# New table of priorities for one large fused kernel (attention, gated feed-forward, routed experts)

## The chip, the cores and the metric

The kernel runs on one core of one Trainium2 chip. The metric is the device time of one execution in microseconds (us). The engines are TensorE (PE, with its weight loads as PEld), VectorE (DVE), ScalarE (ACT), GpSimd (POOL) and SyncE (SP, which issues most transfers).

## What the kernel computes

Three layers in a row, on 2304 tokens. The first is attention by random features, for 4 batches of 8 heads:

```python
q_p, k_p = phi(q * scale), phi(k * scale)   # exp(x @ omega.T - |x|^2/2 - max), 128 features
num = einsum('bhsm,bhmd->bhsd', q_p, einsum('bhsm,bhsd->bhmd', k_p, v))
x = num / (einsum('bhsm,bhm->bhs', q_p, sum_s(k_p)) + 1e-6)      # 2304 x 512
```

The second is a gated feed-forward with 1536 hidden units, and the third sends each token to one of eight experts:

```python
xn = x / rms(x) * rms_g
x = (silu(xn @ w_gate) * (xn @ w_val)) @ w_out                    # 512 -> 1536 -> 512
e = argmax(x @ w_gate2 + bias[modality])                          # and its softmax weight
out = gate_w * (relu(x @ w1[e]) @ w2[e])                          # 512 -> 1024 -> 512
```

## The kernel before

The tokens are worked through in **chunks**. For each chunk PE makes the features (L675), the sums of keys times values (L765) and the numerators with their denominators (L943). DVE divides (L961 to L970). The root of the mean square follows: squares on ACT (L990), the power on POOL (L995, L996), and the scaling of the row either on DVE (L1002, one instruction) or on POOL (L1006 and L1007). The scaled x is then split into a coarse and a fine half-precision part and turned, so that the model dimension lies on the partitions: early chunks by PE (L1320), chunks 4 and later by two transposing transfers that SP issues (L1350). The queries of the later chunks are turned by transfer as well (L624).

**Feed-forward.** The hidden gemm (L1364) fills one half of a PSUM bank of gate and value with twelve matmuls, a *dozen*; two dozens make a unit. Its epilogue is ACT's tanh (L1383), DVE's (tanh+1)*g (L1388) and the product that empties the bank (L1410 on DVE; in early chunks, while the weights come, L1397 on ACT and L1402 on POOL or DVE). The product is split again into a coarse cast (L326 on ACT, L332 on DVE) and a rest (L336), and the output projection (L1434, three matmuls to a triple) reads both. A bank can be filled again only when its L1410 has read it.

**Weights.** In the first 190 us the weights are brought from 64-bit numbers to 32-bit ones and split in two. DVE does the step on the bits in three instructions per tile (L1049, L1056, L1064), and the halves are made by L1028 and L1034 on DVE or ACT. From then on L1028 and L1034 split the weights of the experts, which go out to memory and come back.

**Routing.** Each chunk's logits (L1500, then L1520 to L1542 on DVE) end in its largest expert. Partway through the last chunks the kernel already picks the experts (L1735 to L1762 on DVE, L1771 on PE, L1776 to L1793 on DVE), and after the last it counts ranks and writes a table (L2076, L2089). The experts run with L2312 and L2341 from about 580 us on.

**Spares.** 140 small matmuls on constants (L520), whose results nobody reads, are taken by PE whenever nothing else is ready by the plan.

**What sets the order.** All of this is entered step by step into a `Plan`: each step has an engine (or several to choose from), a planned cost and a wish time `want`. Then `schedule` replays the planned costs and hands every idle engine the ready step of least `want`; that order is what the engines are given, and the chip waits where a step isn't ready in fact. PSUM banks and buffers are given out in the same replay. Before it begins, the rows of `NUDGES` (L55 to L71) shift the wishes:

```python
for first, last, shift, *kind in NUDGES if self.nudged else ():
    for o in self.ops[first : last + 1]:
        if not kind or o.kind in kind:
            o.want += shift
```

A row thus names a range of steps, in the order in which they were entered, a shift, and perhaps one kind of step.

Of the kernel before, what the change touches and what calls it, by code (L numbers as in the profile page):

```python
# [52 lines left out]


NUDGES = (  # L55
    (933, 2761, 6.75, 63), (247, 724, 6.5, 39), (250, 359, -10.75), (0, 1732, 5.5, 7),
    (583, 596, 7.5), (105, 1477, -1.25, 63), (1339, 1364, 3.5), (1353, 1418, 1),
    (1155, 2378, 0.75, 63), (1484, 1548, 1.75), (365, 1101, 17, 32), (2622, 2634, 19.5),
    (713, 744, 14), (1455, 1458, -11.5), (547, 1849, 1.5, 41), (2080, 2406, 17, 40),
    (2046, 2134, 4.5, 41), (1730, 1875, 12.5, 86), (208, 215, -16.75), (1318, 1327, 10),  # L60
    (180, 1260, -1, 9), (123, 857, -9.75, 35), (125, 198, -6.25, 6), (2069, 2083, 1.75),
    (1753, 1763, -7.25), (698, 1599, -8.5, 8), (1925, 3163, 3, 73), (1354, 1356, 20),
    (1397, 1405, 0.25), (2260, 2303, 8.5), (631, 834, 5.25, 21), (145, 174, -3.75, 7),
    (1139, 1184, -5), (489, 494, 8), (2544, 2572, 5), (384, 811, -18.5, 51), (1948, 1977, 5.25, 88),
    (164, 660, -4.25, 29), (1979, 2623, 7, 81), (774, 1927, 3.5, 9), (2252, 2277, -2.75, 80),
    (517, 1281, -2.25, 29), (391, 446, 0.5), (314, 410, -7, 32), (621, 621, -3.5),
    (486, 505, -0.75), (1112, 1113, 8.75), (568, 1395, 0.25, 63), (748, 1137, 3, 9),
    (1402, 1723, -0.5, 87), (183, 1838, -2.5, 28), (1887, 3256, -8, 122), (2241, 2350, -9.5, 41),
    (1442, 1449, -2.5), (1734, 2390, -1.5, 9), (1122, 1126, 7.25), (252, 275, 8.75),
    (2065, 2080, -0.25), (1804, 1873, -1.5, 45), (2515, 2954, 0.75, 63), (2586, 2633, -8),  # L70
)  # L71


# [2388 lines left out]
```

## Time and profile before

| | us |
|---|---|
| median of 3 runs (807.05 to 809.35) | 807.44 |
| time of the profiled execution | 809.51 |
| its span | 807.8 |
| PE busy in the span | 785.0 |
| DVE busy | 564.6 |
| ACT busy | 476.3 |
| POOL busy | 337.5 |

The profiled execution took 1.71 us more than its span, which lies around it, and 2.07 us more than the median. A row that gives a group of instructions has their busy time, the mean of one in ns, and the idle time of the engine just before them with what ended it. In rows in order of time the first number is the start from the beginning of the span, the second how long the stretch of equal instructions took, and a bracket at the end says how long the engine had been idle and which step of which engine ended that.

### The profile page before, as it was taken

The page shows a single profiled execution, that of the slowest core. Times are in us where ns is not written, and L with a number is a line of the kernel's source. Part 1 is how long each engine was busy: PE and PEld are TensorE (multiplying, and loading weights), DVE is VectorE, ACT ScalarE, POOL GpSimd, SP SyncE. Part 2 cuts the span into 40 slices and gives each one's busy share as a digit, 9 for nine tenths or more (in the row PEclk, how much of TensorE's full clock was granted, in tenths as well). Part 3 has the DMA queues.
Part 4 walks back from the last instruction along what each step waited for, and adds up shares of the span by engine and source line. Part 5 has one row for each costly group of instructions (what it writes and reads, how often), then busy time and mean ns, then how long its engine had stood idle before and what let it go on. Part 6 is the DMA issues. An engine that isn't in the chain of part 4 may idle for free.

```text
span 807.8 us, 20366 instructions
## 1 busy us (share of the span) xinstructions
PE 785.0 (97%) x8042; PEld 613.5 (76%) x8042; DVE 564.6 (70%) x1295; ACT 476.3 (59%) x1138; POOL 337.5 (42%) x475
## 2 busy tenths in 40 slices
PE   9999999899999999999999999998999999999995
PEld 8998888788665776877768787777686777777772
DVE  5889899898455889999998999879667222222220
ACT  5767577686635787897877976676242332323231
POOL 0367898664222466545543755322222212222100
PEclk9999999999989999999999999999999999999998
DMA  8436340448213699977789999873826989999960
GB/s 289 166 99 229 112 151 28 131 148 293 82 42 79 184 274 253 277 256 229 248 260 282 265 265 298 269 235 131 320 88 268 405 306 399 415 405 417 418 274 30
DMA packets 69830, 188.25 MB, mean 233 GB/s; under 512 B 36927, under 2 KB 37055, under 8 KB 53856
## 3 DMA queue, kind: packets, MB, share of 16 engines
q1 hardware_dynamic: 66720, 177.27, 65.5%
q0 software_dynamic: 3008, 9.61, 3.1%
q8 instruction: 65, 1.06, 0.5%
q14 instruction: 37, 0.30, 0.1%
HBM read 135.96 MB, written 43.16 MB: 222 GB/s over the span
## 4 chain that ended last, share of the span: by engine, by line
PE 71%; DVE 12%; issue 6%; DMA 4%; POOL 4%; ACT 1%; SPq 0%; POOLq 0%; DVEq 0%; ACTq 0%
PE bank L1364 25%; PE bank L1434 16%; PE bank L2312 8%; PE bank L2341 7%; PE bank L675 4%; PE bank L765 4%; DMA out_dram<-plain,x 2%; DVE big L1028 2%; PE bank L943 2%; PE bank L520 1%; POOL plain L1402 1%; POOL big L336 1%; PE bank L1473 1%; DMA big<-in_w_moe_dram 1%; DVE plain L1388 1%
## 5 line engine op out<-in xcount | busy, mean ns | idle before, releaser
L1364 PE MATMUL bank<-x,big 128*128 128x256 f16 x2592 | 305.9, 273 | 4.7 <-DVE plain L1410 4.4
L1364 PEld LDWEIGHTS <-big 128*128 128x128 f16 x2592 | 251.4, 98 | 49.5 <-issue 7.5
L1434 PE MATMUL bank<-big 128*128 128x512 f16 x648 | 158.0, 382 | 0.0
L336 POOL TENSOR_TENSOR big<-plain,big 128x256 f16<-128x256 f32 (+1 forms) x118 | 107.7, 915 | 110.3 <-ACT big L326 82.6
L1028 DVE SCALAR_TENSOR_TENSOR big<-big,e_fac 128x512 f16<-128x512 f32 x128 | 107.2, 848 | 2.3 <-ACT big L1034 1.5
L1434 PEld LDWEIGHTS <-big 128*128 128x128 f16 x648 | 62.2, 100 | 56.1 <-issue 2.4
L2312 PEld LDWEIGHTS <-big 128*128 128x128 f16 x1632 | 96.0, 98 | 10.6
L2312 PE MATMUL bank<-plain,big 128*128 128x128 f16 x1632 | 101.6, 219 | 0.0
L2341 PE MATMUL bank<-big,plain 128*128 128x512 f16 x408 | 98.5, 379 | 0.0
L1249 ACT ACTIVATE plain<-big,plain 128x1024 bf16<-128x1024 f32 x64 | 73.1, 1142 | 7.0 <-DMA big<-in_w_exp_dram 6.8
L1383 ACT ACTIVATE plain<-bank,w_scale 128x256 f32<-128x256 f32 x108 | 50.9, 473 | 39.8 <-PE bank L1364 27.3
L1034 ACT ACTIVATE big<-big,e_fac 128x512 f16<-128x512 f32 x98 | 68.7, 718 | 1.8 <-DMA split_dram<-big 1.7
L336 DVE TENSOR_TENSOR plain<-plain 128x512 f16<-128x512 f32 (+2 forms) x44 | 28.9, 658 | 57.3 <-ACT plain L326 56.7
L326 ACT CAST big<-plain 128x256 f16<-128x256 f32 (+1 forms) x95 | 39.7, 423 | 44.5 <-DVE plain L1410 26.3
L2341 PEld LDWEIGHTS <-plain 128*128 128x128 f16 x408 | 37.1, 98 | 33.3
L2329 ACT ACTIVATE plain<-bank 128x512 f32<-128x512 f32 x34 | 20.3, 598 | 68.2 <-PE bank L2312 63.3
L692 DVE TENSOR_REDUCE plain<-bank 128x4 f32<-128x512 f32 x71 | 47.3, 682 | 12.1 <-PE bank L675 8.1
L698 ACT ACTIVATE plain<-bank,plain 128x128 f32<-128x128 f32 x164 | 46.0, 376 | 14.6 <-DVE plain L692 14.4
L1388 DVE SCALAR_TENSOR_TENSOR plain<-plain,bank 128x256 f32<-128x256 f32 x108 | 43.9, 412 | 11.5 <-ACT plain L1383 7.7
L336 DVE TENSOR_TENSOR plain<-bank,plain 128x512 f32<-128x512 f32 (+2 forms) x38 | 25.2, 666 | 29.4 <-ACT plain L326 28.9
L326 ACT CAST plain<-bank 128x512 f16<-128x512 f32 (+2 forms) x29 | 16.3, 561 | 42.9 <-PE bank L2312 22.4
L1038 DVE TENSOR_SCALAR plain<-bank,plain 128x512 f32<-128x512 f32 (+1 forms) x12 | 9.0, 748 | 42.9 <-PE bank L2341 28.2
(326 smaller groups left out, 1210.1 us busy)
## 6 DMA issues: line engine op xcount, KB each, us to landing
big<-split_dram SPq DMA_DIRECT2D x60, 1024.0 KB, 16.0
big<-in_w_exp_dram SPq DMA_DIRECT2D x32, 1024.0 KB, 6.7
split_dram<-big SPq DMA_DIRECT2D x32, 1024.0 KB, 7.1
big<-in_w_moe_dram SPq DMA_DIRECT2D x36, 512.0 KB, 4.3
x_dram<-plain SPq DMA_DIRECT2D x18, 258.0 KB, 2.9
plain<-in_v_dram SPq DMA_DIRECT2D x17, 260.0 KB, 3.4
plain<-in_qT_dram SPq DMA_DIRECT2D x14, 256.0 KB, 3.1
plain<-in_kT_dram SPq DMA_DIRECT2D x13, 256.0 KB, 3.8
```

The source lines that it names most:

```text
L326: nc.scalar.mul(out, src, factor) if factor != 1.0 else nc.scalar.copy(out, src)
L336: eng.tensor_tensor(out=out, in0=src, in1=hi, op=ALU.subtract)
L692: lambda: nc.vector.tensor_reduce(out=mx.tile, in_=pp.tile, axis=AX.X, op=ALU.min),
L1028: nc.vector.scalar_tensor_tensor(out=out, in0=src, scalar=factor, in1=hi, op0=ALU.mult, op1=ALU.subtract)
L1034: nc.scalar.activation(out, src, AF.Copy, scale=factor)
L1249: lambda c=c, h=h, cs=cs: nc.scalar.activation(junk.tile, raws[c][:, cs], AF.Square, bias=tiny, accum_out=sums[:, 2 * c + h : 2 * c + h + ...
L1364: nc.tensor.matmul(gv[:, t, :], w[a][:, kk, :], self.x[x][:, kk, :], start=kk == 0 and m == 0, stop=kk == KD - 1 and m == 2,)
L1383: lambda: nc.scalar.activation(th.tile, gv[:, 0, :], AF.Tanh, scale=one(BACK)),
L1388: lambda: nc.vector.scalar_tensor_tensor(out=th.tile, in0=th.tile, scalar=1.0, in1=gv[:, 0, :], op0=ALU.add, op1=ALU.mult,),
L1434: nc.tensor.matmul(self.acc[j].tile, h[:, a, r], out_w[f][:, i, :], start=f == 0 and m == 0, stop=f == FT - 1 and m == 2,)
L2312: nc.tensor.matmul(ph[:, j, :], w_of(c, p, k * F2 + (4 * n + j) * P, P), x[a][:, kk, :], start=kk == 0 and j == 0 and m == 0, stop=kk == K ...
L2341: nc.tensor.matmul(y.tile, hs[n][a][:, kk, :], w_of(2 + n, p, kk * DM, DM), start=f == 0 and m == 0, stop=f == KF2 - 1 and m == 2,)
```

## The change

`NUDGES` has 149 rows in place of 61; two of them were there before. The first lines of the difference stand for all:

```diff
 NUDGES = (
-    (933, 2761, 6.75, 63), (247, 724, 6.5, 39), (250, 359, -10.75), (0, 1732, 5.5, 7),
-    (583, 596, 7.5), (105, 1477, -1.25, 63), (1339, 1364, 3.5), (1353, 1418, 1),
...
+    (933, 2761, 6.75, 63), (225, 710, 6.75, 39), (257, 357, -12.5), (0, 1732, 6, 7),
+    (584, 598, 8.25), (105, 1477, -1.25, 63), (1336, 1362, 3.5), (1353, 1410, 1),
...
```

Nothing else is edited. The steps are the same ones with the same operands; their order on the engines, the banks and buffers they are given, and for 93 steps the engine that does them, come out differently. Since the table is longer, every later line of the kernel has a number 22 higher: L1410 of the kernel before is L1432 of the changed one. Three places show what moved. In the rows `bank_90` to `bank_97` are the eight PSUM banks.

**DVE, where the experts are first picked** (544 to 560 us in the trace of before). The kernel before:

```order
L1742 TENSOR_REDUCE xs<-xs 128x16
L1762 CAST xs<-xs 128x1
L1535 TENSOR_SCALAR plain<-plain 128x1
L1536 RECIPROCAL plain<-plain 128x1
L1537 TENSOR_SCALAR plain<-plain 128x512
L1539 TENSOR_SCALAR plain<-plain 128x1
L1542 MEMSET plain 128x3
L1028 SCALAR_TENSOR_TENSOR big<-big,e_fac 128x512
L1388 SCALAR_TENSOR_TENSOR plain<-plain,bank_93 128x256
L1388 SCALAR_TENSOR_TENSOR plain<-plain,bank_95 128x256
L1410 SCALAR_TENSOR_TENSOR plain<-bank_93,w_scale,plain 128x256
L1410 SCALAR_TENSOR_TENSOR plain<-bank_95,w_scale,plain 128x256
```

The changed kernel, from the same place in the listing (L1410 and L1432 are here what L1388 and L1410 are above, L1757 to L1784 the picks L1735 to L1762, L1557 the step L1535):

```order
L1410 SCALAR_TENSOR_TENSOR plain<-plain,bank_93 128x256
L1280 TENSOR_REDUCE plain<-plain 128x1
L1050 SCALAR_TENSOR_TENSOR big<-big,e_fac 128x512
L1432 SCALAR_TENSOR_TENSOR plain<-bank_93,w_scale,plain 128x256
L1757 TENSOR_TENSOR xs<-logits,lmax 128x128
L1761 TENSOR_TENSOR xs<-xs 128x128
L1764 TENSOR_REDUCE xs<-xs 128x16
L1784 CAST xs<-xs 128x1
L1410 SCALAR_TENSOR_TENSOR plain<-plain,bank_95 128x256
L1037 TENSOR_SCALAR e_near<-bank_90 128x1
L1432 SCALAR_TENSOR_TENSOR plain<-bank_95,w_scale,plain 128x256
L1557 TENSOR_SCALAR plain<-plain 128x1
```

The pair of steps that empties bank 3 stood behind the picks and stands ahead of them now, and the pair for bank 5 has moved ahead of L1535 and what follows it.

**PE, at the numerators of one chunk** (458 to 470 us). Each row stands for all its repeats in a row: 12 of L943, 3 of each L1434, and of L1364 24 on bank 3, then 12 each on banks 5, 1, 5, 1 and 2. The kernel before:

```order
L943 MATMUL bank_94<-plain 128x65
...
L1434 MATMUL bank_96<-big 128x512
...
L1434 MATMUL bank_97<-big 128x512
...
L1364 MATMUL bank_93<-x_528,big 128x256
...
L1364 MATMUL bank_95<-x_528,big 128x256
...
L1364 MATMUL bank_91<-x_528,big 128x256
```

The changed kernel (L965 is L943, L1386 is L1364, L1456 is L1434), with 12 of each L1386 in a row and 3 of each L1456; the two rows on bank 1 stand on either side of the chunk's twelve route matmuls:

```order
L965 MATMUL bank_94<-plain 128x65
...
L1386 MATMUL bank_91<-x_526,big 128x256
...
L1456 MATMUL bank_96<-big 128x512
...
L1456 MATMUL bank_97<-big 128x512
...
L1386 MATMUL bank_95<-x_526,big 128x256
...
L1456 MATMUL bank_97<-big 128x512
...
L1386 MATMUL bank_95<-x_526,big 128x256
...
L1456 MATMUL bank_96<-big 128x512
...
L1386 MATMUL bank_92<-x_526,big 128x256
```

Where 84 hidden matmuls stood in a row, dozens of them now take turns with triples of the output projection.

**DVE, at the end of the weight stage** (182 to 190 us), where L1049, L1056 and L1064 make the last tiles of weights. The kernel before:

```order
L336 TENSOR_TENSOR big<-plain,big 128x256
L1402 TENSOR_TENSOR plain<-plain,big 128x256
L332 CAST big<-plain 128x256
L1388 SCALAR_TENSOR_TENSOR plain<-plain,bank_95 128x256
L1049 TENSOR_SCALAR big<-big 128x512
L1402 TENSOR_TENSOR plain<-plain,big 128x256
L1056 SCALAR_TENSOR_TENSOR big<-big 128x512
L1064 SCALAR_TENSOR_TENSOR big<-big 128x512
L1049 TENSOR_SCALAR big<-big 128x512
L336 TENSOR_TENSOR x_528<-bank_90,x_528 128x4x128
L1056 SCALAR_TENSOR_TENSOR big<-big 128x512
L1064 SCALAR_TENSOR_TENSOR big<-big 128x512
```

The changed kernel, up to the same last L1064 (L1071, L1078 and L1086 are L1049, L1056 and L1064, L714 is the row maximum L692, L358 is L336):

```order
L1086 SCALAR_TENSOR_TENSOR big<-big 128x512
L714 TENSOR_REDUCE plain<-bank_93 128x4
L1071 TENSOR_SCALAR big<-big 128x512
L1078 SCALAR_TENSOR_TENSOR big<-big 128x512
L1086 SCALAR_TENSOR_TENSOR big<-big 128x512
L358 TENSOR_TENSOR x_526<-bank_90,x_526 128x4x128
L1071 TENSOR_SCALAR big<-big 128x512
L1078 SCALAR_TENSOR_TENSOR big<-big 128x512
L1086 SCALAR_TENSOR_TENSOR big<-big 128x512
```

The early epilogue (L1388, L1402 and the split that follows) no longer stands between these steps; it comes after them, or is done by POOL and ACT.

Some moves are told in words. At 145 us in the trace of before, where PE waits for the first queries to be divided and turned, 24 spares stand in runs of 7, 7 and 10; in the changed kernel 27 stand there, in runs of 11, 9 and 7. The four groups of L765 on 64 rows, two of which lie at 225 and 228 us before, have little other work between them in the changed kernel. For chunk 7 the scaling of x is done by POOL (L1006, L1007) in place of DVE (L1002), and between the numerators of that chunk and the first hidden gemm that reads its turned x stand 6 dozens and 8 triples in place of 8 dozens and 7 triples and some smaller work. For the last chunk the rank count's matmul has less of PE's work ahead of it. PE's order is the same at 82 to 130 us, from about 262 to 404, from 410 to 424, from 581 to 602 and from 609 to 628 us.

## Rows read from the trace of the kernel before

**Rows 1.** The page: the span and each engine's busy time.
```profile
span 807.8 us, 20366 instructions
PE 785.0 (97%) x8042; PEld 613.5 (76%) x8042; DVE 564.6 (70%) x1295; ACT 476.3 (59%) x1138; POOL 337.5 (42%) x475
```
**Rows 2.** PE's instructions grouped by line; columns as told above.
```profile
L1364 PE MATMUL bank<-x,big 128*128 128x256 f16 x2592 | 305.9, 273 | 4.7 <-DVE plain L1410 4.4 <-ACT big L1034 0.3
L520 PE MATMUL bank<-ones_w,ones_h 128*128 128x252 bf16 x140 | 20.3, 287 | 2.6 <-DVE plain L970 1.3 <-DVE plain L462 1.3
```
**Rows 3.** Stretches: us, then PE, PEld, DVE, ACT, POOL busy (instructions), clock, DMA, GB/s.
```profile
130.00:190.00 60.00, 57.41 (x578) 50.98 (x577) 56.18 (x117) 44.28 (x121) 38.02 (x50) 1.00 0.39 122
262.00:425.00 163.00, 161.28 (x1537) 121.44 (x1535) 152.63 (x360) 130.58 (x304) 87.86 (x113) 1.00 0.84 247
425.00:580.00 155.00, 151.01 (x1345) 116.67 (x1344) 136.40 (x346) 108.23 (x236) 64.20 (x96) 0.99 0.83 252
580.00:798.00 218.00, 216.21 (x2798) 162.82 (x2796) 70.65 (x171) 63.95 (x119) 45.30 (x60) 1.00 0.82 327
798.00:807.80 9.80, 0.00 (x0) 0.00 (x0) 0.00 (x0) 0.69 (x1) 0.98 (x1) 0.69 0.09 30
```
**Rows 4.** Chain of waits, 100 to 200 us: start, us, what.
```profile
144.80 1.15 DVE big L1064
```
**Rows 5.** PE in order of time, 138 to 153 us.
```profile
146.70 0.63 PE L1320 MATMUL bank<-ident,plain 128*128 128x128 f32 x4 [1.01 <-DVE plain L961]
...
150.92 0.27 PE L520 MATMUL bank<-ones_w,ones_h 128*128 128x252 bf16 x1 [1.12 <-DVE plain L970]
```
**Rows 6.** DVE in order of time, 176 to 190 us.
```profile
181.47 0.42 DVE L1388 SCALAR_TENSOR_TENSOR plain<-plain,bank 128x256 f32<-128x256 f32 x1
...
182.44 1.23 DVE L1402 TENSOR_TENSOR plain<-plain,big 128x256 f32<-128x256 f32 x1 [0.18 <-ACT big L1034]
...
188.79 0.69 DVE L1064 SCALAR_TENSOR_TENSOR big<-big 128x512 uint32<-128x512 uint32 x1
```
**Rows 7.** PE in order of time, 452 to 467 us.
```profile
460.37 2.78 PE L1364 MATMUL bank<-x,big 128*128 128x256 f16 x24
464.80 2.45 PE L1364 MATMUL bank<-x,big 128*128 128x256 f16 x21 [1.64 <-DVE plain L1410]
```
**Rows 8.** DVE in order of time, 456 to 467 us.
```profile
464.27 0.48 DVE L1410 SCALAR_TENSOR_TENSOR plain<-bank,w_scale,plain 128x256 f32<-128x256 f32 x1
```
**Rows 9.** PE in order of time, 544 to 560 us.
```profile
556.12 4.05 PE L1364 MATMUL bank<-x,big 128*128 128x256 f16 x21 [2.33 <-DVE plain L1410]
```
**Rows 10.** DVE in order of time, 544 to 560 us.
```profile
552.45 0.29 DVE L1735 TENSOR_TENSOR xs<-logits,lmax 128x128 f32<-128x128 f32 x1
...
555.59 0.87 DVE L1410 SCALAR_TENSOR_TENSOR plain<-bank,w_scale,plain 128x256 f32<-128x256 f32 x2
...
558.81 0.29 DVE L1746 TENSOR_TENSOR xs<-xs 128x128 bf16<-128x128 f32 x1
```
**Rows 11.** The two stretches at half clock; columns as in Rows 3.
```profile
228.40:235.10 6.70, 6.70 (x25) 4.26 (x25) 3.54 (x19) 1.78 (x5) 1.02 (x2) 0.50 0.27 79
556.10:559.40 3.30, 3.28 (x16) 2.35 (x16) 3.09 (x13) 2.35 (x5) 1.29 (x2) 0.50 0.70 283
```
**Rows 12.** SP's queue in order of time, 464 to 479 us.
```profile
467.38 6.92 SPq L1350 DMA_TRANSPOSE x<-big  x2
```
**Rows 13.** PE in order of time, 474 to 479 us.
```profile
477.60 1.58 PE L1364 MATMUL bank<-x,big 128*128 128x256 f16 x13
```
**Rows 14.** POOL's and DVE's scaling of x, grouped by line.
```profile
L1006 POOL TENSOR_SCALAR plain<-plain 128x512 f32<-128x512 f32 x14 | 12.3, 878 | 0.9
L1007 POOL TENSOR_TENSOR plain<-plain 128x512 f32<-128x512 f32 x14 | 20.5, 1465 | 1.2
...
L1002 DVE SCALAR_TENSOR_TENSOR plain<-plain 128x512 f32<-128x512 f32 x4 | 5.3, 1317 | 0.0
```
**Rows 15.** PE in order of time, 612 to 622 us.
```profile
619.15 0.25 PE L2089 MATMUL bank<-x,xs 128*128 128x62 bf16 x3 [1.75 <-DVE x L2076]
```

48 rows, old and new, of the table NUDGES are left out of this document.

## Prediction

> **What bounds the kernel now.** I read the page first, then the stretches, then in each stretch PE's rows in order of time. PE is busy for 785.0 of 807.8 us [rows 1], so 22.8 us of it are idle: about 1.3 before the first matmul, 9.8 behind the last one while the last output leaves [rows 3], and 11.7 in waits between. Of the busy time 20.3 us are the 140 spares, which feed nothing [rows 2]; where a spare stands ahead of ready work it costs stream, and where it stands in a wait it costs nothing. No edit of the order alone can win much more than these 11.7 us, a part of the spares, and what the clock took.
>
> Stretch by stretch the limit differs [rows 3]. To about 190 us the weights are being made: the chain of waits runs over POOL and, from about 117 us, over DVE's bit steps [rows 4], and DVE is busy for 56.18 of the 60 us from 130 to 190. From 262 us PE is the bound, with 1.72 us idle in 163, then 3.99 in 155 (425 to 580), then 1.79 in 218 (580 to 798). DVE is close behind to 580 us (152.63 of 163, 136.40 of 155) and then falls to 70.65 of 218, so that the experts are PE's alone.
>
> The waits that are worth naming: 1.01 and 1.12 us at 146 and 150, for DVE's division [rows 5]; 1.64 at 464.8, where a hidden gemm wants a bank that DVE's L1410 empties only at 464.27 [rows 7, 8]; 2.33 at 556.1, the same wait, with the first picks of the experts ahead of the L1410 on DVE [rows 9, 10]; 1.75 at 619, for the table [rows 15]. PE's list as a whole puts 4.4 us down to L1410 [rows 2]. Twice the granted clock fell to 0.50, the 1.2 GHz level: from 228.4 to 235.1 without any idle PE before it, and from 556.1 to 559.4 right behind the 2.33 us of idleness [rows 11]. At half speed a stretch of busy PE takes twice its time, so the first cost about 6.70 / 2 = 3.35 us and the second 3.30 / 2 = 1.65.
>
> **The change, part by part.** No step is added or taken away, so each part is a wait that goes, comes or moves. 93 steps change engine; priced at the means of their rows they take 3.8 us off DVE and put 4.3 on ACT and 0.5 on POOL. No engine's total decides by that: DVE's 564.6 and ACT's 476.3 are far from the span [rows 1].
>
> *Head, 0 to 82 us.* Seven spares fewer, at some 0.108 us each (the spacing of a run of them), are 0.8 us of stream less; against that ACT's steps now stand closer to their readers. I put this at nothing, with 1 us to either side.
>
> *End of the weight stage, 130 to 190.* Here DVE is the bound. The work listed on DVE up to the last L1064, which ends at 189.5 [rows 6], falls from 292 instructions and 160.9 us to 289 and 158.1, by the sum of their rows' durations: epilogue pieces such as the L1388 at 181.47 and the L1402 at 182.44 [rows 6] now stand behind it or go to ACT and POOL. If all of DVE's relief came through, PE would get 2.8 us; but DVE also has 3.8 us idle here, PE waits only 2.59 [rows 3], and three spares more are issued at 145. The upper end is therefore 1.8, the lower 0, and I take the middle, 0.9: the waits at 146 and 150 end at DVE's division [rows 5], which the removed epilogues don't precede.
>
> *The clock at 228.* The four 64-row groups of L765 are moved closer together. The rows show the fall with a PE that was never idle [rows 11]; a fall in the changed kernel is as likely as here, so I count nothing, with 1.7 (half of the 3.35) both ways.
>
> *The wait at 464.* Before, 84 hidden matmuls stand in a row, of which the first 24 run from 460.37 [rows 7]. They want fresh banks faster than DVE empties them. In the changed kernel every dozen or two is followed by a triple or two, at about 0.65 us a triple, and the bank that is reused next has 5.97 us of other PE work between its filling and its reuse. The bank wait ends 0.53 us after the start of the L1410 at 464.27 [rows 7, 8]. I count the full 1.64 us as gained; what is late next there is the same L1410 by some tenths.
>
> *The wait at 556.* Before, DVE does L1735, L1739, L1742, L1762, the softmax pieces L1535 to L1542 and an L1028 from 552.45 on, and empties banks 3 and 5 only from 555.59 on [rows 10]. In the changed kernel bank 3 is emptied ahead of the picks and bank 5 ahead of L1535. The waiting gemm's lead, PE work between the filling of its bank and its reuse, grows from 0.06 to 4.31 us; the epilogue that frees the bank is a tanh, an L1388 and an L1410, the last two of 0.42 and 0.43 us [rows 6, 10]. I count 2.33 us as gained, and the 1.65 us of the clock with it, since that fall directly follows the wait [rows 9, 11]. The price stands behind: the picks come later on DVE. Before, the last steps of the picks end at 559.1 [rows 10], and no PE work waits for them soon.
>
> On that clock the Trainium skill, page "TensorE: Matmul & The Clock Gate", section "A second HAM failure mode: psum-queue depth-cycling", holds that short idle gaps between groups of matmuls, as banks are cycled, make the clock swing and cost throughput. By this rule the finer alternation in the changed kernel would be a danger wherever its leads fail. The trace agrees at 556 only: it shows waits of 1.64 us at 464 without a fall [rows 3, 7], and a fall at 228 without a wait [rows 11].
>
> *What stays.* PE's order around the wait at 619 is unchanged, and DVE's lead for the table as well: 1.75 us stay [rows 15]. So do two waits, at 319 and 413 us, that make up nearly all of the 1.72 idle from 262 to 425 [rows 3].
>
> *New waits.* Three places lost lead. The rank matmul has 4.57 us of PE work ahead of it for a chain of small DVE steps, 0.29 us the largest [rows 10], that sums to 5.31: about 0.7 us. One output triple behind the hidden gemms has 4.34 us for an epilogue of five steps; the two on DVE take 0.42 and 0.43 [rows 6, 10], so that it waits only where they queue, at a guess between nothing and the 1.64 that such a queue cost at 464 [rows 7]. And the turned x of chunk 7 (below) has 14.5 us of PE work where it had 16.8. Before, DVE scales, SP's two transposes run from 467.38 to 474.3, and the first reader starts at 477.60 [rows 12, 13], so 3.3 us are spare; 2.3 less of lead and a scaling on POOL of 878 + 1465 ns in place of DVE's 1317 [rows 14], 1.0 more, take 3.3, so it just holds; late by as much again, it would wait 2. None of the three can gain, since none of these places waits now. Together they lie between 0 and some 4.3 us; I take 1.2, near the lower end: the 0.7 of the rank and a half, since the rows leave the last just in time.
>
> **Sum.** From the profiled execution's own 809.51: 0.9 + 1.64 + 2.33 + 1.65 = 6.5 less, 1.2 more, which is 804.2. That execution lies 2.07 above the median of 807.44. If this comes from a fall of the clock that the median runs don't have, part of the 1.65 isn't there to be gained, and if it comes from what the profile adds, all of it comes off again: between 802.1 and 804.2 for the median I take 803.5, 0.5% under 807.44.
>
> **The rivals.**
>
> *Given back elsewhere, about 806.5.* The planned costs that make this order are not the chip's, so waits that go at two places may come at others. For it: DVE has 18.6 us free in 425 to 580 [rows 3], and each wait there is for DVE; a gain of 4 us in PE's waits makes PE ask for each bank 4 us sooner. Half of the gains of 425 to 580, (1.64 + 2.33 + 1.65) / 2 = 2.8, would go: 803.5 + 2.8 = 806.3, with a little of the new waits 806.5. Against it: the L1410 rows are late by place in DVE's list, not for lack of DVE time.
>
> *More is gained, about 799.5.* The stage's relief comes in full (1.8), no new wait bites (1.2), and the clock doesn't fall at 228 either (half of 3.35): 803.5 - 0.9 - 1.2 - 1.7 = 799.7. Against it: all three must hold.
>
> *Slower, about 811.* The turned x of the late chunks comes too late. A step later on POOL moves SP's transposes, and behind them in SP's queue wait the queries' transposes and the weights' parts; the 6.92 us of the two transposes [rows 12] is then exposed in part. It decides from the point at which the transposes land after the first reader, 3.3 us later than now. A wait of some 4 us at chunk 7 and again at one further chunk, one with the clock at half speed behind it at 1.65 [rows 11], adds 9.7; with the gain of the DVE order at 556 kept that is 803.5 + 9.7 - 2.3 = about 811. Against it: the lead of the other late chunks hardly changed.
>
> **How the numbers follow.** Forecast 0.55, given back 0.27, more gained 0.10, slower 0.08. The least that a measurement of this kernel can tell from no change is about 0.3%, 2.4 us. Below 805.0 lie most of the forecast's case (0.50 of 0.55), all of "more" and a little of "given back": 0.62. Within 805.0 to 809.9 lie most of "given back" and a rest of the others: 0.28. Above: 0.10, the slower case and the tail of "given back". The range takes in the head's 1 us and the clock's 1.7 below, 799.5, and above it reaches past "given back" to 808.5.
>
> **What would show it.** Right: no PE wait over 0.5 us behind L1432 (the renumbered L1410) in 425 to 580, and PE idle there under 2.5 us in place of 3.99 [rows 3]; no stretch at 0.50 in 540 to 580; the last L1086 before 188 us. Wrong: a PE wait of over 2 us at the first reader of a late chunk's turned x with the DMA as its releaser; a bank wait elsewhere in 425 to 580 of the size of those that went; or a new stretch at half clock in the first 262 us.

## The result, and the profile after

The changed kernel takes 801.15 us (median of 20 runs, 798.14 to 810.75) beside 808.74 for the kernel before (20 runs, 806.44 to 813.07). The ratio is 0.9907 with a 95% interval of 0.9882 to 0.9932: 0.9% faster, 7.5 us. The forecast was 803.5 and faster; the direction is right, the time lies in the range, and the gain against the median shown then was put at 3.9 us, about half of what came.

The profiled execution took 799.23 us, 10.28 less than that of the kernel before. Its first two lines on the page stand against [rows 1]:

```profile
span 797.5 us, 20359 instructions
PE 778.8 (98%) x8042; PEld 610.2 (77%) x8042; DVE 562.1 (70%) x1294; ACT 480.6 (60%) x1143; POOL 341.4 (43%) x474
```

The span is 10.3 us shorter while PE is busy for 6.2 us less and idle for 4.1 less. The matmuls are the same, so less busy time means matmuls that ran faster: no stretch of this profile but its end was at half clock, and half clock cost the profile before about 5.0 us of busy time. The other 1.2 us lie at the very start, where the first matmuls (L668) end at 9.22 us in the profile of before and at 7.98 here. That is no matter of the order: in a second profile of each kernel they end at 8.26 and at 9.64. These are the rows of the kernel before from 5 us on, in its first and in its second profile:

```profile
4.79 4.43 PE L668 MATMUL bank<-om,big 128*128 128x128 f32 x31
```

```profile
4.75 3.51 PE L668 MATMUL bank<-om,big 128*128 128x128 f32 x30
```

The stretches, with the columns of [rows 3] and ends that move with the kernel's pace:

```profile
130.00:190.00 60.00, 58.66 (x588) 52.45 (x587) 52.52 (x115) 43.96 (x120) 36.10 (x46) 1.00 0.47 151
262.00:421.00 159.00, 157.96 (x1516) 119.92 (x1515) 148.43 (x350) 128.56 (x297) 88.10 (x112) 1.00 0.88 256
421.00:573.00 152.00, 151.85 (x1345) 116.53 (x1343) 135.84 (x341) 110.64 (x239) 68.81 (x100) 1.00 0.88 266
```

The third line is the one to read. PE's 1345 matmuls are, all but some twenty at either end, those of 425 to 580 before. As many take 152 us instead of 155, with PE idle for 0.15 us instead of 3.99, while DVE is busy for about as long as before (135.84 and 136.40). In the first line DVE has 3.66 us less to do within the same 60 us, and PE's idle time falls from 2.59 to 1.34.

PE in order of time at the two places of the prediction, to be held against [rows 7, 9]:

```profile
457.31 2.11 PE L1456 MATMUL bank<-big 128*128 128x512 f16 x9
459.25 1.47 PE L1386 MATMUL bank<-x,big 128*128 128x256 f16 x12
460.56 0.81 PE L1456 MATMUL bank<-big 128*128 128x512 f16 x3
461.20 1.47 PE L1386 MATMUL bank<-x,big 128*128 128x256 f16 x12
...
541.76 0.45 PE L1522 MATMUL bank<-route_w,plain 128*128 128x24 bf16 x12
542.07 2.78 PE L1386 MATMUL bank<-x,big 128*128 128x256 f16 x24
...
546.78 0.17 PE L1793 MATMUL bank<-xs 128*128 128x1 bf16 x1
546.81 2.78 PE L1386 MATMUL bank<-x,big 128*128 128x256 f16 x24
549.43 0.81 PE L1456 MATMUL bank<-big 128*128 128x512 f16 x3
550.07 1.47 PE L1386 MATMUL bank<-x,big 128*128 128x256 f16 x12
551.38 0.22 PE L1828 MATMUL bank<-xs 128*128 128x128 bf16 x1
```

No row has a bracket: neither bank wait is there. The table's wait is, as it was at 619 [rows 15]; the largest waits that PE has left are

```profile
PE bank L2111 <- DVE x L2098: 1.7, 1, 1.7
PE bank L542 <- DVE plain L992: 1.3, 1, 1.3
PE bank L542 <- DVE plain L484: 1.3, 1, 1.3
```

(line and releaser, us in total, times, longest).

Where the time went can be read off matmuls that stand at the same place in both orders. How much earlier they start in the changed kernel:

| in the profile of before | earlier by | what lies between |
|---|---|---|
| 151.0 | 1.83 | head and weight stage; 1.2 of it the start (above) |
| 248.6 | 5.44 | the half clock of 228.4 to 235.1 |
| 320.9 | 5.80 | a shorter wait for a turned query |
| 526.9 | 7.34 | the wait at 464.8 |
| 581.0 | 11.57 | the wait at 556.1 and its half clock |
| end of the span | 10.3 | 0.9 given back among the experts, 0.4 behind the last matmul |

### The profile page after: what moved, and what is told of

Read it like the earlier page. It is cut to its first block, busy times and chain, and to the rows that moved or that the text cites. A ratio compares the mean times of both kernels' runs of the same rounds, so it can differ in the third digit from the quotient of the medians.

```text
span 797.5 us, 20359 instructions
## 1 busy us (share of the span) xinstructions
PE 778.8 (98%) x8042; PEld 610.2 (77%) x8042; DVE 562.1 (70%) x1294; ACT 480.6 (60%) x1143; POOL 341.4 (43%) x474
## 4 chain that ended last, share of the span: by engine, by line
PE 78%; issue 6%; DVE 6%; POOL 4%; DMA 4%; ACT 1%; POOLq 0%; DVEq 0%; SPq 0%; ACTq 0%
PE bank L1386 29%; PE bank L1456 15%; PE bank L2334 8%; PE bank L2363 7%; PE bank L697 4%; PE bank L787 3%; DMA out_dram<-plain,x 2%; PE bank L965 2%; PE bank L542 2%; POOL plain L1424 1%; DMA plain<-big 1%; DVE big L1050 1%; POOL big L358 1%; PE bank L1495 1%; PE bank L2193 1%
## 5 line engine op out<-in xcount | busy, mean ns | idle before, releaser
L1386 PE MATMUL bank<-x,big 128*128 128x256 f16 x2592 | 305.4, 273 | 0.5 <-DVE plain L1432 0.3
L1386 PEld LDWEIGHTS <-big 128*128 128x128 f16 x2592 | 250.0, 98 | 42.7 <-issue 2.0
L1456 PE MATMUL bank<-big 128*128 128x512 f16 x648 | 155.7, 379 | 0.0
L358 POOL TENSOR_TENSOR big<-plain,big 128x256 f16<-128x256 f32 (+1 forms) x115 | 104.0, 908 | 93.0 <-ACT big L348 56.5
L1050 DVE SCALAR_TENSOR_TENSOR big<-big,e_fac 128x512 f16<-128x512 f32 x128 | 110.2, 873 | 0.5
L1456 PEld LDWEIGHTS <-big 128*128 128x128 f16 x648 | 62.0, 99 | 55.8 <-DVE plain L1410 0.2
L2334 PE MATMUL bank<-plain,big 128*128 128x128 f16 x1632 | 99.6, 219 | 0.6 <-issue 0.6
L2363 PE MATMUL bank<-big,plain 128*128 128x512 f16 x408 | 96.6, 379 | 0.0
L358 DVE TENSOR_TENSOR plain<-plain 128x512 f16<-128x512 f32 (+2 forms) x45 | 29.4, 660 | 70.5 <-ACT plain L348 55.0
L1056 ACT ACTIVATE big<-big,e_fac 128x512 f16<-128x512 f32 x103 | 71.9, 718 | 2.1 <-DMA split_dram<-big 1.5
L714 DVE TENSOR_REDUCE plain<-bank 128x4 f32<-128x512 f32 x72 | 48.0, 683 | 14.7 <-PE bank L697 11.1
L1410 DVE SCALAR_TENSOR_TENSOR plain<-plain,bank 128x256 f32<-128x256 f32 x108 | 43.7, 412 | 10.6 <-ACT plain L1405 7.0
L358 DVE TENSOR_TENSOR plain<-bank,plain 128x512 f32<-128x512 f32 (+2 forms) x38 | 25.1, 665 | 29.6 <-ACT plain L348 29.4
L1424 POOL TENSOR_TENSOR plain<-plain,big 128x256 f32<-128x256 f32 x30 | 30.8, 1028 | 18.0 <-ACT big L1056 10.9
L720 ACT ACTIVATE xs<-bank,plain 128x128 f32<-128x128 f32 x108 | 30.7, 385 | 10.9 <-DVE plain L714 10.8
```

Source lines behind the costliest of these rows:

```text
L358: eng.tensor_tensor(out=out, in0=src, in1=hi, op=ALU.subtract)
L714: lambda: nc.vector.tensor_reduce(out=mx.tile, in_=pp.tile, axis=AX.X, op=ALU.min),
L720: nc.scalar.activation(ph[:, h, :], pp[:, h, :], AF.Exp, bias=mx[:, h : h + 1], scale=-1.0)
L1050: nc.vector.scalar_tensor_tensor(out=out, in0=src, scalar=factor, in1=hi, op0=ALU.mult, op1=ALU.subtract)
L1056: nc.scalar.activation(out, src, AF.Copy, scale=factor)
L1386: nc.tensor.matmul(gv[:, t, :], w[a][:, kk, :], self.x[x][:, kk, :], start=kk == 0 and m == 0, stop=kk == KD - 1 and m == 2,)
```

## Experiments

Two of the kernels take the two tables apart; most others move one or a few steps by hand in the finished order, with everything else as it was. The theory of the prediction is that the gain is that of the two bank waits of 425 to 580. Its rivals are that it comes from the early part, or from the clock alone.

The first four kernels below ran on one chip, all others on a second one, each beside the kernel before. Runs with a mean clock of 0.996 or more are taken as runs without a half-speed stretch ahead of the end: the profiles without one have 0.995 to 0.997, those with one 0.984 to 0.995. In such runs the kernel before takes 807.3 us on the first chip (mean of 15) and 804.6 on the second (mean of 20). So medians of the two chips are not compared with each other, and the changed kernel itself was not run on the second.

### Half of the table each

```diff
-for first, last, shift, *kind in NUDGES if self.nudged else ():
+for new, (first, last, shift, *kind) in [(t is NUDGES_1, r) for t in (NUDGES_1, NUDGES_2) for r in t if self.nudged]:
     for o in self.ops[first : last + 1]:
-        if not kind or o.kind in kind:
+        if (o.n < CUT) == new and (not kind or o.kind in kind):
             o.want += shift
```

In the first kernel `NUDGES_1` is the new table, `NUDGES_2` the old one and `CUT` 1400; in the second they are the old one, the new one and 1800. From about 262 us on PE's listing is then, row by row and but for four spares before 346 us, that of the kernel before in the first and that of the changed kernel in the second.

> The changed table for the steps below number 1400, the old one for the rest: PE's order is the changed kernel's to about 260 us, and from there word for word that of the kernel before. The two profiles lie 5.1 us apart at 262 us. Theory A (the first part gains by DVE's relief in the weight stage, and the missing half-speed stretch at 228 is chance): some 1.8 us over the kernel before in a run without the fall in either, up to 5.1 where only the kernel before has it; the waits of 1.64 us at about 464 and 2.33 at about 556 are there as before, with a half-speed stretch behind the second. Theory B (all the gain lies in 425 to 580): no gain, within 0.3%. Theory C (the new L765 order keeps the clock up): 5 us faster, no half-speed stretch near 225.

Measured: ratio 0.9999 (0.9975 to 1.0023), median 808.52. Nothing is gained, which speaks against theory C.

> The old table for the steps below number 1800, the changed one for the rest: PE's order is that of the kernel before to about 260 us, and from there the changed kernel's. Theory A and B (the bank waits of 425 to 580 are what goes): 1.64 + 2.33 + 1.65 (the clock behind the second wait) + about 0.7 at 319, some 6 us faster than the kernel before; PE idle from 425 to 580 under 0.5 us. Theory C' (the order of the first part is needed, since its earlier weights feed the second): under 3 us.

Measured: ratio 0.9914 (0.9884 to 0.9944), median 801.93. Nearly all of the gain is there. The stretch of the waits in this kernel, and below it the same stretch in a further profile of the kernel before:

```profile
425.00:575.00 150.00, 149.85 (x1331) 115.17 (x1330) 134.95 (x340) 109.90 (x236) 66.88 (x98) 1.00 0.87 264
```

```profile
425.00:575.00 150.00, 145.66 (x1306) 111.97 (x1304) 132.06 (x341) 105.30 (x230) 62.97 (x95) 1.00 0.82 247
```

PE idles for 0.15 us against 4.34, and both are at full clock throughout. So the later part of the order pays, by waits that go, and does so without a fall of the clock on either side.

In the first kernel the weight stage did gain:

```profile
130.00:190.00 60.00, 58.65 (x588) 52.48 (x587) 52.50 (x115) 43.69 (x120) 36.37 (x46) 1.00 0.44 147
```

PE is busy for 58.65 of 60 us as in the changed kernel, and at 243 us its matmuls start 0.7 us before those of the kernel before. But the waits of 1.88 and 2.33 us at 460 and 551 are there, and behind the second one the clock fell:

```profile
551.00:554.40 3.40, 3.40 (x17) 2.42 (x17) 3.19 (x13) 2.33 (x5) 1.30 (x2) 0.50 0.68 275
```

That costs 1.7 us, more than the 0.7 gained. In the 12 runs of this kernel the mean clock was never above 0.995, where spans without a fall reach 0.997; so its gain of about a microsecond can't be seen in its time.

### The two kernels again

> The kernel before, unchanged, for a second profile and the granted clock of more runs. If the half-speed stretches at 228 and 556 belong to this order, both are there again and its runs have a mean clock of about 0.99; if the one at 228 comes by chance, it is missing in some runs and these are about 3.4 us shorter.

Measured: ratio 1.0016 (0.9991 to 1.0041), which shows what the comparison makes of no change. The profile has a span of 804.0 us and full clock at both places:

```profile
226.50:233.20 6.70, 6.70 (x41) 3.95 (x39) 4.91 (x25) 1.96 (x6) 1.55 (x3) 1.00 0.30 79
551.50:555.00 3.50, 3.18 (x32) 2.73 (x32) 3.29 (x14) 2.35 (x5) 1.30 (x2) 1.00 0.66 267
```

against 0.50 in [rows 11]. Yet the wait is the same:

```profile
551.56 2.78 PE L1364 MATMUL bank<-x,big 128*128 128x256 f16 x24 [2.33 <-DVE plain L1410]
554.60 0.22 PE L1806 MATMUL bank<-xs 128*128 128x128 bf16 x1 [0.26 <-DVE xs L1746]
```

The same order with the same wait thus runs with and without the fall. Against this profile, which has no fall but that of the end either, the changed kernel's span is 6.5 us shorter. By the starts of the same matmuls it is 1.1 us to 243 us, 1.7 more to 522 us, 3.1 more to 575 us, and 0.7 behind. That last part is hardly the order's: among the experts this profile has 1.6 us of waits for ACT's L2329 that the first profile of the same kernel doesn't have.

> The changed kernel, unchanged. Its profile had no half-speed stretch before the end. If that belongs to the order, a second profile has none either and its runs spread under 1%; if falls come by chance, single runs have a lower mean clock and are longer by half of the half-speed time.

Measured: ratio 0.9919 (0.9887 to 0.9951). This profile, of 800.9 us, has one fall, at the L787 groups (the L765 of before):

```profile
232.50:235.90 3.40, 3.40 (x14) 2.20 (x14) 1.60 (x10) 1.58 (x5) 1.23 (x3) 0.51 0.27 81
```

So the fall near 228 is no trait of the old order: it comes in both, and not in every run of either. To compare without it, the means of those runs of these four kernels whose clock was 0.996 or more: 807.3 us for the kernel before (15 of 43 runs), 801.6 for the later half of the new order (7 of 8), 800.1 for the changed kernel (3 of 12). The later part is worth 5.7 us at equal clock, the first 1.5 on top of it. Only a third of the runs of the kernel before are in this class and 7 of 8 of the later half, so the medians hold some of the clock as well; and the mean of the changed kernel is one of three runs only.

### One place by hand: the wait at 556

Is the wait made by the order on DVE, as the prediction has it, or by the place on PE? In the kernel before, steps are taken from the finished order and put behind another one:

```diff
+MOVES = (
+    ([2751, 2622, 2623], 2646),
+    ([2752], 2669),
+    ([2631, 2632], 2634),
+    ([2754], 2679),
+)
-        for o in self.schedule():
+        for o in moved(self.schedule()):
```

Row 1 puts DVE's early picks and the softmax pieces behind the L1410 of bank 5, row 2 the pick's matmul behind the waiting dozen, row 3 two triples behind the dozen on bank 3, and row 4 the rank matmul behind two more dozens. The first kernel has rows 1 and 2, the second row 3, the third rows 1 to 3, the fourth all.

> The kernel before, with one thing moved: on DVE the early picks and the softmax pieces (L1735 to L1542 at 552.45 to 554.3) stand behind the L1388 and L1410 of banks 3 and 5 instead of ahead of them, and the matmul of the pick (L1771) stands behind the dozen that waits. If the order of DVE made the wait, as the prediction has it, it falls from 2.33 us to nearly nothing. If PE's lead of 0.06 us made it, the chain tanh, L1388, L1410 still has to run after the dozen: DVE's L1410 can start some 0.6 us earlier and no more, and 1.6 to 1.8 us of the wait stay.

Measured: ratio 1.0013 (0.9991 to 1.0036), no change. PE in order of time:

```profile
550.87 1.47 PE L1364 MATMUL bank<-x,big 128*128 128x256 f16 x12 [1.84 <-DVE plain L1410]
552.78 0.16 PE L1771 MATMUL bank<-xs 128*128 128x1 bf16 x1 [0.44 <-DVE plain L1535]
...
555.37 0.22 PE L1806 MATMUL bank<-xs 128*128 128x128 bf16 x1 [1.10 <-DVE xs L1746]
```

The wait is 0.5 us shorter, near the 1.6 to 1.8 that were to stay if PE's lead made it, and the picks that now stand behind it make PE wait 0.44 and 1.10 us elsewhere: 3.38 us in all, where it was 2.33 + 0.26.

> The kernel before, with one thing moved: on PE the two output triples (L1434, 1.3 us) that stand ahead of the dozen on bank 3 stand behind it, so that the lead of the next dozen on that bank is 1.4 us instead of 0.06. If the lead alone made the wait it falls from 2.33 to about 1 us. If DVE's order holds the bank anyway (its L1410 comes at 555.59 behind the picks), the wait stays 2.3 us.

Measured: ratio 1.0017 (0.9988 to 1.0046); the wait stays at 2.33 us, as if DVE's order held the bank:

```profile
552.73 2.78 PE L1364 MATMUL bank<-x,big 128*128 128x256 f16 x24 [2.33 <-DVE plain L1410]
```

> The kernel before with both moves: picks behind the L1410 rows on DVE, and the two triples behind the dozen on PE. If the two causes hide each other, the wait falls to 1.0 us or less, that is by more than the two single moves gain together, and the half-speed stretch behind it is missing in the profile; the kernel is 1.3 to 2 us faster at equal clock.

Measured: ratio 1.001 (0.9983 to 1.0038). The bank wait falls to 1.11, a tenth more than expected, which neither move did alone, and most of what it gave comes back at the rank matmul:

```profile
553.56 1.47 PE L1364 MATMUL bank<-x,big 128*128 128x256 f16 x12 [1.11 <-DVE plain L1410]
...
557.87 0.22 PE L1806 MATMUL bank<-xs 128*128 128x128 bf16 x1 [1.39 <-DVE xs L1746]
```

The expectation of 1.3 to 2 us at equal clock was wrong: 1.11 + 1.39 is 2.50, as much as before, and the runs at a clock of 0.996 or more take 804.7 us (3 of 10) like those of the kernel before in that set (15 of 31). The fall of the clock is missing here, as expected.

> The kernel before with both moves at 556 us (picks behind the L1410 rows on DVE, two triples behind the dozen on PE) and a third: the rank matmul (L1806) stands two more dozens later on PE. If the chain from the route matmul over DVE's picks to the rank matmul is too long for the PE work that lies between, the 1.39 us that came up at L1806 with both moves go, about 1.1 us of the bank wait stay, and the waits of the place sum to 1.1 instead of 2.6. If DVE's time is what is short, a wait of the same size comes up at the next bank.

Measured: ratio 0.9979 (0.9957 to 1.0001). With two more dozens ahead of it the rank matmul waits no longer, and no other wait takes its place:

```profile
550.33 1.47 PE L1364 MATMUL bank<-x,big 128*128 128x256 f16 x12 [1.11 <-DVE plain L1410]
...
555.71 0.22 PE L1806 MATMUL bank<-xs 128*128 128x128 bf16 x1
```

DVE's time isn't short here, then. Two chains run from PE over DVE and back, one that empties a bank and one from the route matmul over the picks to the rank matmul, and they share DVE within some 9 us. Whichever goes first delays the other. What takes the waits away is PE work between the ends of both. The time doesn't tell this kernel from no change: the interval holds 1, and at a clock of 0.996 or more it takes 803.5 us (2 of 10 runs) beside 804.3 (5 of 28).

### One place by hand: the wait at 464

```diff
+MOVES = (
+    ([2294], 2293),
+)
```

Step 2294 is the L1410 at 464.27, and 2293 its L1388.

> The kernel before, with one instruction moved: the L1410 that starts at 464.27 stands directly behind its own L1388 (458.99) instead of 5 us later. The wait of 1.64 us at 464.8 goes, and PE's stream from there on is 1.3 to 1.6 us earlier; where the wait comes back within 10 us at the next bank, the plan is short of DVE time there and not of order.

Measured: ratio 1.001 (0.9983 to 1.0037). PE in order of time:

```profile
455.90 4.09 PE L1364 MATMUL bank<-x,big 128*128 128x256 f16 x36
461.13 5.07 PE L1364 MATMUL bank<-x,big 128*128 128x256 f16 x45 [1.14 <-DVE plain L1410]
```

One dozen gets through (36 in place of 24 in a row), and then PE waits 1.14 us at the next bank. The dozen starts 1.6 us earlier than in the second profile of the kernel before, the one behind it 0.3. The second case of the expectation holds in its first half: the wait came back. Whether DVE's time or its order behind that point is short, this run doesn't tell.

### Undoing it in the changed kernel

```diff
+MOVES = (
+    ([2246, 2247, 2297, 2298], 2364),
+)
```

> The changed kernel with one thing undone at about 457 us: four output triples stand behind the two dozens on bank 5 instead of ahead of them, so that four dozens follow each other. If the alternation of dozens and triples is what took the wait at 464 away, a wait of about 1.1 us for L1432 comes back at the first dozen on bank 5, since that L1432 ends at 458.43 in the profile and PE asks at 457.3. If DVE's order did it, no wait comes.

Measured: ratio 0.9945 (0.9917 to 0.9973). In its profile the head ran at half clock (last section), so that the place lies 12 us later:

```profile
467.72 1.47 PE L1386 MATMUL bank<-x,big 128*128 128x256 f16 x12
470.19 2.78 PE L1386 MATMUL bank<-x,big 128*128 128x256 f16 x24 [1.00 <-DVE plain L1557]
472.81 1.46 PE L1456 MATMUL bank<-big 128*128 128x512 f16 x6
```

A wait of 1.00 us is back at the first dozen on bank 5. The step that the trace names as releaser, L1557, starts 0.39 us behind DVE's L1432 of that bank (469.66), which ends at 470.14 and is the one PE needs:

```profile
469.66 0.48 DVE L1432 SCALAR_TENSOR_TENSOR plain<-bank,w_scale,plain 128x256 f32<-128x256 f32 x1
```

So without the alternation with triples 1.00 us of the wait is there. Whether the alternation alone, put into the kernel before, would take its 1.64 away was not tried.

```diff
+MOVES = (
+    ([2754], 2753),
+)
```

> The changed kernel with the rank matmul (L1828) moved ahead of a dozen, a triple and a dozen (3.3 us of PE work). If the PE work between route and rank is what hides DVE's chain of picks, PE waits about 1.3 us at L1828, since DVE's last step of the chain ends at 549.4 and PE is there at 548.1. If the chain is short enough anyway, there is no wait.

Measured: ratio 0.9955 (0.9926 to 0.9985), with

```profile
551.03 0.22 PE L1828 MATMUL bank<-xs 128*128 128x128 bf16 x1 [1.21 <-DVE xs L1768]
```

as expected. The changed kernel's DVE order alone does not hide the picks; the 9.6 us of PE work from the route matmul at 541.76 to the rank at 551.38 do. Before, 8.6 us lay between them (545.99 to 554.60 in the second profile), of which 2.6 were waits.

### The table's wait

```diff
-                lambda: rest(nc.vector, lo.tile, pt.tile, hi.tile),
+                lambda n=len(plan.ops): rest(nc.gpsimd if n == 2837 else nc.vector, lo.tile, pt.tile, hi.tile),
+MOVES = (
+    ([2843], 2841),
+)
```

> The changed kernel with the wait for the table taken on: one rest (L358, the step that starts at 607.42) is done by POOL, which is idle there, in place of DVE, and six output matmuls of an expert (L2363, 1.3 us) that need it stand ahead of the table's matmul instead of behind it. If the table's wait of 1.7 us is only DVE's length there, it falls to 0.4 us and the kernel is 1.3 us faster at equal clock, 0.16%; if POOL's rest is late (0.9 us and its queue), the wait moves to L2363.

Measured: ratio to the kernel before 0.9889 (0.9863 to 0.9915), median 799.04. In order of time:

```profile
608.77 2.75 PE L2363 MATMUL bank<-big,plain 128*128 128x512 f16 x12
612.45 0.25 PE L2111 MATMUL bank<-x,xs 128*128 128x62 bf16 x3 [0.93 <-DVE x L2098]
```

The wait falls from 1.71 to 0.93 us, so 0.8 of the 1.3 was gained; the table itself came 0.5 us later against the matmuls ahead of it, for which I have no cause. Whether the kernel is faster by it than the changed kernel is not shown: that one was not run on this chip. Against the kernel before on the same chip it is faster by 1.1%, but part of this is the clock, which was 0.996 or more in 3 of its 6 runs and in 5 of 28 of the kernel before. In these it takes 798.8 us beside 804.3, 5.5 less; the changed kernel was 7.2 less on its own chip. So only the wait in the profile speaks for keeping it.

## Why the prediction was right, and where it wasn't

**What bounds it.** Right. The gain is in the waits of the stretch 425 to 580; PE idles there for 0.15 us, where under 2.5 was the mark set.

**The wait at 464**, 1.64: right in size (PE gains 1.49 and 1.60 us by the two profiles of before, between the end of the common order near 422 us and the next place that both orders share, at 526.9) and in cause as far as tested: without the alternation of dozens and triples 1.00 us comes back.

**The wait at 556**, 2.33: the size was right (3.1 us between 522 and 575 without any fall of the clock, of which 2.33 are this wait and 0.26 the rank matmul's; the cause of the other 0.5 isn't shown), but the step that explained it failed in its weight. The prediction put the late L1410 down first of all to the picks ahead of it on DVE, and named the lead on PE beside it. Moving the picks alone gained nothing in time; the lead on PE of both chains had to grow, and the changed kernel has both. "No PE work waits for them soon" was wrong for the order before, where the rank matmul waits 0.26 us and any delay of the picks comes out there.

**The clock behind it**, 1.65: counted as certain, and it is a chance. It fell in two of five profiles with this wait of 2.33 us. The correction from the profiled run to the median, which allowed for part of that, was a guess that took off 0.7 us; the profile turned out 0.8 above the median of 20 and not 2.07, so the guess came near by luck.

**The weight stage**, 0.9: right within its bounds. DVE's last L1086 ends at 185.2 us in place of 189.5, PE gained 1.2 us within the stretch and 1.1 to 243 us, and runs at equal clock say 1.5 for the first part as a whole.

**The clock at 228**, nothing: not refuted. The fall came there in one of eight profiles with the old order of that place (for 6.8 us) and in two of six with the new (3.4 and 6.8), too few to tell the two apart. The two profiles that happened to be compared differ by 3.4 us there, a third of their difference.

**New waits**, 1.2: mis-sized, the three places measured none. The rank matmul was put at 0.7, from 4.57 us of PE work against a chain of 5.31. The work is there (546.81 to 551.38), but the chain took half as long: from the start of the pick's matmul at 546.78 to the end of DVE's last step

```profile
549.14 0.29 DVE L1768 TENSOR_TENSOR xs<-xs 128x128 bf16<-128x128 f32 x1
```

it is 2.65 us. The turned x of chunk 7 came in time, as the rows had it. Outside these places PE waits a little longer ahead of 130 us: 0.8 us at L863 where it was 0.5 at L841, and 0.9 at L1126 where it was 0.4 at L1104.

**The wait at 319** was held to be unchanged. It fell from 1.14 to 0.43 between the two profiles compared:

```profile
320.94 0.54 PE L943 MATMUL bank<-plain 128*128 128x65 f16 x12 [1.14 <-DMA plain<-big]
```

```profile
315.14 0.54 PE L965 MATMUL bank<-plain 128*128 128x65 f16 x12 [0.43 <-DMA plain<-big]
```

Its releaser is a transfer, and it differs from execution to execution: 0.6 to 1.3 us in the profiles with the old later order, at most 0.43 in four with the changed one, and 1.09 and 1.04 in the other two (the kernels with four triples moved and with the table's wait taken on). So these 0.7 us are no sure gain.

**The sum.** Without the 1.2 us of new waits and with 0.8 more at 556, the 6.5 less 1.2 become 7.3, near the 7.5 measured; but 1.65 of them are the clock's, which is chance. Without it 5.6 us are left, where the two profiles without a fall differ by 6.5, of which 0.7 among the experts are hardly the order's, and the runs at equal clock by 7.2. So up to 1.6 us of the gain are not accounted for. Of the 3.6 us by which the gain was put too small, 1.3 come from the median shown then, 807.44, which lay that much below the median of 20 runs, and 2.0 from the new waits and the second wait. The sum of the rival "slower" has a slip: its 2.3 for the order at 556 is taken off a second time, as 803.5 holds it already; without that it is about 813.

"Given back elsewhere" is what three of the moves by hand did (the two with the picks behind the bank's steps, and the one at 464), and what the searched order avoided. "More gained" gave the profiled run's time (799.7 and 799.23) without its reasons: its clock at 228 is chance. The sign of being wrong that names the first 262 us is missing in the profile compared; a later profile of the changed kernel with one move has a half-speed stretch at 18.7 us, where no profile of the kernel before has one (last section).

## What to carry to other kernels

A wait for a bank names the step that came last, but that step often can't come sooner without pushing another chain back on the same engine: before counting the wait as a gain, list every chain that crosses the engine within the next ten microseconds and ask for the lead of each. What hides such chains is work of the bound engine that needs none of them, spread between their ends: the place at 556 was mended only by moves on both engines. And a term taken from one profile's clock is worth what a second profile of the same kernel confirms.

## What the runs showed of the hardware

**The granted clock falls in some executions of an order and not in others.** Behind the wait of 2.33 us at 551 to 556 it fell to half for 3.4 us in two of five profiles. Behind a wait of 2.08 us that ended at 462.1 it fell in one profile, and behind one of 2.09 us in another it did not. At the groups of L765 near 230 us, where PE is never idle, it fell in three of the fourteen profiles, for 3.4 or 6.8 us, under both orders. The table's wait, 1.7 us in all profiles but that of the kernel which takes it on, never had a fall behind it. How often a run has no fall before the end differs: 15 of 43 runs of the kernel before on the first chip, 15 of 31 and 5 of 28 in two sets on the second, 7 of 8 with the later half of the new order, none of 12 with its first half. What sets these odds stays open. The Trainium skill, page "TensorE: Matmul & The Clock Gate", section "A second HAM failure mode: psum-queue depth-cycling", says of one kernel that frequent short idle times between groups of matmuls, as PSUM banks are cycled, make the clock swing. The trace agrees that a gap can be followed by a fall, and shows single falls and not a swing: in both profiles of the changed kernel the stretch from 421 us on, with the finest alternation of banks, has none before the end.

**One fall early on lasted longer.** In the profile of the kernel with four triples moved, PE waited 1.79 us at 16.8 us for a load of values, and then ran at half clock for 20.5 us, against full clock in the changed kernel's profile (the second row):

```profile
18.70:39.20 20.50, 20.50 (x109) 20.16 (x110) 9.35 (x24) 8.05 (x27) 0.00 (x0) 0.50 0.53 178
```

```profile
18.70:39.20 20.50, 20.50 (x222) 19.40 (x220) 16.52 (x45) 16.58 (x56) 5.31 (x11) 1.00 0.51 178
```

109 matmuls in place of 222: about 10 us. In two other profiles with this head PE waited 0.35 and 0.95 us for the same load, and the clock did not fall. The head of that kernel is the changed kernel's, whose runs have a mean clock under 0.990 in 6 of 32, at 809.4 to 810.8 us; the profiles don't show these runs, so that they had the same fall is inferred from their clock. The kernel before has none in over a hundred. The new head has 11 spares between 5 and 20 us where the old one has 15, and so asks for the values sooner. That this makes such runs likelier fits, but it is argued and not shown: the kernel with the new head and the old rest has none in 12 runs, and the one with the old head and the new rest none in 8.
